# Two new step orders in the attention of an attention + squared-ReLU FFN kernel, with the spread sums as a step of their own and one head's scaled output by VectorE

## The chip, the cores and the metric

The kernel runs on one core of one Trainium2 chip. The metric is the device time of one execution in microseconds (us). Before the change three runs gave 1317.71, 1319.16 and 1319.85 us; the median is 1319.16 us. The core has five engines with an instruction queue each, which they work off strictly in order: TensorE (PE in the profile; PEld is its weight load), VectorE (DVE), ScalarE (ACT), GpSimd (POOL) and SyncE (SP), which here only issues DMAs. An instruction that needs another engine's result waits at the head of its queue, and all behind it waits too.

## The reference

Thresholded attention over 8 batches x 8 heads, 576 positions, head size 64, and then a two-layer FFN on 4608 tokens of width 512 with a hidden layer of 2048, all in float32:

```python
scores = scale * np.matmul(q, k.transpose(0, 1, 3, 2))
thresh = np.max(scores, axis=-1, keepdims=True) - tau
scores = np.where(scores >= thresh, scores, -1000000000.0)
scores = scores - np.max(scores, axis=-1, keepdims=True)
attn = np.exp(scores)
attn = attn / (np.sum(attn, axis=-1, keepdims=True) + 1e-09)
x = np.matmul(attn, v)            # heads of one batch side by side: (4608, 512)
h = np.maximum(x @ w_in, 0.0)
out = h * h @ w_out
```

The two weight arrays come in as 64-bit floats, so the kernel also turns them into 32-bit ones, with integer operations.

## The kernel before, in words

**Stages.** The attention fills the first 523 us of the profiled execution. The FFN follows; its layers use sums of blocks (a fast matrix product in two levels) and are not touched by the change.

**The unit of the attention** is one tile of 128 query rows of two heads (`units`, 144 of them; in two of nine, the 64 rows left over of two head pairs share a tile). Two units, A and B, make a period; there are 72 periods and a few more to fill and empty the pipeline. Each period does these steps; a step's name is the one in the order lists:

- `SA`, `SB`: score products of a unit with the first 512 keys, line 434 with 512 columns, in 64x64 tiles of TensorE. `RA`, `RB`: with the 64 keys left over, line 434 with 64 columns. They go to six PSUM banks of one tile `sc`: unit A to banks 0 and 5 and parts of 1 and 4, unit B to banks 2 and 3 and other parts of 1 and 4.
- `topA0` ... `topB1`: VectorE copies one head's 576 scores out of PSUM with the extremum (line 452). `leastA/B`: GpSimd makes the threshold (line 459). `powA0` ...: ScalarE's exponential (line 462). `maskA0` ...: VectorE's compare, multiply and row sum (line 467). `over`, `inv`: the sums plus 1e-9 on GpSimd (line 474) and their reciprocal on VectorE (line 477).
- `V`, `W`, `U`: TensorE transposes the masked weights, 64 rows at a time (line 380, tile form 64x128): 8 blocks of 18 in `V`, 2 in `W`, 8 in `U`, which is 16, 4 and 16 instructions. `V` and `U` go to the one two-bank PSUM buffer `pt`, `W` to banks 2 and 3 of `sc`. `W` also spreads the reciprocal sums over the rows with 8 small products (line 515, tile form 64x64). `eV`, `eW`, `eU`: ScalarE copies them out to SBUF (line 523).
- `PV`: the product with the values (line 532, tile form 64x64, 36 products of 128 columns, or the same in pieces), into banks 0 and 5. `x`: ScalarE copies the two heads' results out (line 658, 128x128 each). `xm`: GpSimd multiplies both by the spread reciprocal sums (line 664, 128x256), and SyncE stores them to DRAM.
- `T`: transposes of later queries (8 instructions) or keys (10), line 398, tile form 64x128, to the middles of banks 1 and 4, in most periods. `eT`: ScalarE takes them out (lines 403 and 411), and the next loads of queries or keys are issued.
- `c1` ... `c6`, `fetch`: the conversion of one block of FFN weights (line 205 on ScalarE, 212, 219 and 245 on GpSimd, 227 and 235 on VectorE) and its load. `s1`, `s2`: block sums of the first layer's weights on GpSimd.

**What sets the order.** Nothing schedules these steps: two lists written by hand, `CONVERTING` for the periods that convert weights (numbers 2 to 34) and `PLAIN` for the later ones, give the order in which every engine's queue receives them. Each `-` behind a name means one period earlier, so one pass of the list works on several periods at once. `run_period` walks a list; `BEGIN_WITH` has the lists of the first two periods. Between instructions on the same PSUM bank by different engines, `touch` adds a wait, even where they do not overlap. All instructions on a resource keep the order of the list.

Of the kernel before, what the change touches and what calls it, by code (L numbers as in the profile page):

```python
# [13 lines left out]
ALU = mybir.AluOpType  # L14
# [34 lines left out]
def kernel(  # L49
# [25 lines left out]
    nc = tc.nc  # L75
    B, H, S, D = q.shape
    P = 128
# [7 lines left out]
    BANK = 512  # L85
# [19 lines left out]
    ident = const.tile([P, P], FP32, name="ident")  # L105
# [168 lines left out]
    HALF = P // 2  # L274
# [80 lines left out]
    def touch(what, made, at, size, key=0):  # L355

        if at is None:
            return
        on = range(at // BANK, (at + size - 1) // BANK + 1)
        met = {made.ins.engine}  # L360
        for kind, other, others, its in reversed(touched):
            e = other.ins.engine
            if e == made.ins.engine:
                continue
            if on[-1] < others[0] or others[-1] < on[0]:
                if any({what, kind} == {x, y} and any((key - its) % n == 0 for n in rings) for x, y, rings in MEET):
                    continue
                tc.declare_no_dep(made.ins, other.ins, reason="other banks")
            elif e not in met:
                met.add(e)  # L370
                tc.add_manual_dep(made.ins, other.ins.name, behind, reason="same bank")
        touched.append((what, made, on, key))
        while len(touched) > 300:
            touched.popleft()

    def half_turn(pt, slot, of, at=None):

        for r in range(2):
            rows = ds(r * HALF, HALF)
            made = nc.tensor.transpose(pt[:, r, ts(slot, HALF)], of[rows, :], ident[rows, rows])  # L380
            touch("turns", made, at and at + r * BANK, BANK)
# [39 lines left out]
    soft, given, smalls = {}, deque(), {}  # L421
# [63 lines left out]
    wT = {}  # L485

    TURNS = {}
    for g in range(2, 2 * len(pairs)):
        two, x = divmod(g - 4, 4)
# [3 lines left out]
    FILLS = {"V": (0, 8), "W": (8, 2), "U": (10, 8)}  # L493
    SCALE_AT = 10
# [4 lines left out]
    def fill(m, f, pt, at=None):  # L499

        first, count = FILLS[f]
        if m not in wT:
            wT[m] = sb.tile([P, (2 * CH + 2) * P], FP32, tag="wT", bufs=W_RING, name="wT")
        for i, (u, c) in enumerate(FIRST[first : first + count]):
            half_turn(pt, i, weights[2 * m + u][:, c, :, :].rearrange("p j d -> p (j d)"), at)
        if f == "W":
            rs = smalls.pop(m)
            for j in range(2):
                for r in range(2):
                    rows = ds(r * HALF, HALF)  # L510
                    for u in range(2):
                        one = rs[rows, 3, 2 * u + j : 2 * u + j + 1]
                        wide = bass.AP(tensor=one.tensor, offset=one.offset, ap=[one.ap[0], [0, D]])
                        to = pt[ds(u * D, D), r, ts(count + j, HALF)]
                        made = nc.tensor.matmul(to, wide, ident[rows, rows], start=True, stop=True)
                        touch("turns", made, at and at + r * BANK, BANK)

    def filled(m, f, pt, at=None):

        first, count = FILLS[f]  # L520
        count += 2 * (f == "W")
        to = wT[m][:, ds(weight_at(first) * P, count * P)]
        touch("weights", nc.scalar.copy(joined(to), whole(pt, 0, count)), at, 2 * BANK, m)  # L523
# [35 lines left out]
    def has(n):  # L559
        return 0 <= n < NU  # L560
# [22 lines left out]
    def converts(p):  # L583
        return is_wide and (has_chunk(p) or has_chunk(p - 1))

    def has_chunk(p):
        return p in starts

    def begun(n):
        return starts.get(n)  # L590

    FIRST_PERIOD = -2
    PLAIN = """
        PV-- x-- V-- eV-- RA- c1- c3- inv-- W-- xm-- eW-- powB1-- c2 maskA0-- SA- maskA1-- U- c4 topA0- s1--
        powB0-- topA1- leastA- SB- eU- maskB1-- c6 RB- T- s2 maskB0-- eT- over- topB0- powA0- topB1- c5
        powA1- leastB- fetch
    """.split()
    CONVERTING = """
        RB- maskA0-- SA- maskA1-- inv-- powB1-- W-- U- topA0- eW-- c6- fetch topA1- leastA- SB- maskB0-- c1-
        c3- eT- maskB1-- topB0- c4 over- topB1- c2- leastB- eU- powA1- powA0- PV- c5 V- x- RA powB0- eV- T  # L600
        xm- s1 s2
    """.split()

    BEGIN_WITH = {
# [2 lines left out]
        maskB0 maskB1  # L607
        """.split(),
        1: """
        fetch SA RA RB SB T eT over topA0 topA1 leastA inv V topB0 topB1 leastB powA0 powA1 eV W powB0 eW  # L610
        maskA0 maskA1 powB1 maskB0 maskB1
        """.split(),
    }
# [7 lines left out]
    def period(p):  # L621

        A, B_, a, b = 2 * p, 2 * p + 1, 2 * p - 2, 2 * p - 1
        m, turns = p - 2, TURNS.get(p, ())
        late, pt = {"W": []}, {}

        def fills(f, m):
            if has(2 * m):
                pt[f] = pt_pool.tile([P, 2, BANK], FP32, tag="pt", name="pt")
                fill(m, f, pt[f])  # L630

        def evict(f, m):
            if has(2 * m):
                filled(m, f, pt[f], 2 * BANK if f == "W" else None)

        def W():
            if has(2 * m + 2):
                pt["W"] = middle()
                fill(m + 1, "W", pt["W"], 2 * BANK)

        def turn_some():
            free = None
            if turns and p < 2:
                pq = pt_pool.tile([P, 2, BANK], FP32, tag="pt", name="pq")
                free = [(pq[:, r, :], None) for r in range(2)]
            late["turn"] = [turn(g // 2, g % 2, free or spots()) for g in turns]

        def PV():
            if has(2 * m):
                values(m)  # L650

        def values_out():
            if not has(2 * m):
# [24 lines left out]

        def every(key):
            for then in late.get(key, ()):  # L680
                then()

        steps = {
            "U": lambda: fills("U", m), "V": lambda: fills("V", m + 1), "W": W, "T": turn_some,
            "eU": lambda: evict("U", m), "eV": lambda: evict("V", m + 1), "eW": lambda: evict("W", m + 1),
            "eT": lambda: every("turn"),
            "SA": lambda: scored(A), "SB": lambda: scored(B_),
            "RA": lambda: scored_rest(A), "RB": lambda: scored_rest(B_),
            "PV": PV, "x": values_out, "xm": given_out,
            "c1": lambda: convert1(begun(p)), "c2": lambda: convert2(begun(p)),  # L690
            "c3": lambda: convert3(begun(p)), "c4": lambda: convert4(begun(p - 1)),
            "c5": lambda: convert5(begun(p - 1)), "c6": lambda: convert6(begun(p - 1)),
            "s1": lambda: sums_due(p) and sums_step(), "s2": lambda: sums_due(p) and p < 60 and sums_step(), "fetch": lambda: fetch(begun(p + 2)),
        }
# [127 lines left out]
    both = arena[:, ds(X_AT[1], 2 * X_SIZE)].rearrange("p (s z) -> p s z", s=2)  # L822
# [525 lines left out]
```

## Time and profile before

| what | value |
|---|---|
| median of three runs | 1319.16 us (1317.71 to 1319.85) |
| the profiled execution's own time | 1316.8 us |
| its span, first to last instruction | 1315.0 us, so 1.8 us lie around it |
| TensorE's granted clock, mean | 0.997 |
| busy share of the span: PE, DVE, ACT, POOL | 98%, 75%, 65%, 78% |
| converting stretch, 33 to 250 us: PE, DVE, ACT, POOL busy | 211.64, 206.37, 202.92, 196.95 of 217 us |
| plain stretch, 264 to 490 us: the same | 225.91, 192.34, 205.80, 178.14 of 226 us |
| FFN, 523 to 1315 us: the same | 783.10, 526.75, 388.01, 621.13 of 792 us |

A busy TensorE in this table is not TensorE at its peak: its instructions are pipelined, and the end of each is modelled. Where one instruction starts against the one before it says more than the share.

### The profile page before, as it was taken

To read this page: it belongs to the slowest core of one execution; us is meant where nothing else is said; L and a number is where in the kernel's file an instruction comes from. 1 tells how busy PE (TensorE), PEld (TensorE's weight loads), DVE (VectorE), ACT (ScalarE), POOL (GpSimd) and SP (SyncE) were. 2 spreads that over 40 slices of the span, in tenths; PEclk is the share of its full clock that TensorE was granted. 3 is DMA by queue.
4 is the path that set the end of the run, shared out by engine and by line. 5 is a ranking of instruction groups with operands and counts; after the bars stand their busy time and mean duration, and the time that the engine had idled before them with its cause. 6 is when DMAs were issued, how large, how long until landed. Compare 5 with 4: busy or idle time off the path is not lost.

```text
span 1315.0 us, 46033 instructions
## 1 busy us (share of the span) xinstructions
PE 1292.6 (98%) x18287; PEld 1108.5 (84%) x18287; DVE 983.6 (75%) x2345; ACT 856.6 (65%) x1576; POOL 1030.5 (78%) x1070
## 2 busy tenths in 40 slices
PE   8999999999999999999999999999999999999998
PEld 5666666677777777988888888999999999999998
DVE  6999999988888886787786877867656654665463
ACT  6999999999999897476666766765524322432240
POOL 3989899888888653698897997958777777777775
PEclk8999999999999999999999999999999999999999
DMA  6655666443333311576768767769754134513511
GB/s 164 170 146 152 158 192 183 119 98 99 82 74 84 74 45 36 164 229 174 221 187 228 214 179 213 212 234 367 273 161 161 56 107 161 161 57 106 161 33 33
DMA packets 291417, 196.23 MB, mean 149 GB/s; under 512 B 100097, under 2 KB 252161, under 8 KB 291201
## 3 DMA queue, kind: packets, MB, share of 16 engines
q1 hardware_dynamic: 289888, 192.87, 51.0%
q8 instruction: 144, 2.36, 0.8%
q14 instruction: 73, 0.59, 0.1%
q10 hardware_dynamic: 1312, 0.41, 0.1%
HBM read 120.85 MB, written 72.35 MB: 147 GB/s over the span
## 4 chain that ended last, share of the span: by engine, by line
PE 54%; DMA 3%; ACT 2%; DVE 1%; issue 1%; SPq 1%; POOL 0%; ACTq 0%; DVEq 0%; POOLq 0%
PE po L1082 28%; PE ph L940 15%; PE ph L947 10%; DVE arena L125 1%; DMA g<-arena 1%; DMA wall<-w 1%; ACT c L796 1%; DMA arena<-xT 1%; SPq L778 1%; ACT arena L909 0%; DMA w<-arena 0%; ACT arena L910 0%; DVE arena L122 0%; PE sc L532 0%; ACT arena L523 0%
## 5 line engine op out<-in xcount | busy, mean ns | idle before, releaser
L125 POOL TENSOR_TENSOR arena<-arena 128x512 f32<-128x512 f32 (+1 forms) x314 | 378.0, 1222 | 138.0 <-DVE arena L125 107.8
L1082 PE MATMUL po<-wall,arena 128*128 128x128 f32 x3528 | 395.1, 275 | 2.3 <-ACT arena L757 2.0
L1082 PEld LDWEIGHTS po<-wall,arena 128*128 128x128 f32 x3528 | 394.4, 192 | 2.9 <-ACT arena L757 2.4
L125 DVE TENSOR_TENSOR arena<-ph,arena 128x512 f32<-128x512 f32 x378 | 255.3, 689 | 86.3 <-PE ph L940 30.7
L122 POOL TENSOR_TENSOR arena<-arena 128x128 f32<-128x128 f32 (+1 forms) x322 | 265.6, 827 | 25.3 <-DMA arena<-w 9.0
L940 PE MATMUL ph<-arena,wall 128*128 128x256 f32 x1176 | 256.8, 380 | 3.0 <-DVE arena L125 2.5
L940 PEld LDWEIGHTS ph<-arena,wall 128*128 128x128 f32 x1176 | 222.0, 190 | 37.4 <-DVE arena L125 7.6
L452 DVE TENSOR_SCALAR_CACHE_REDUCE arena<-sc 128x576 f32<-128x576 f32 x288 | 208.4, 753 | 51.0 <-ACT arena L523 36.3
L125 DVE TENSOR_TENSOR arena<-po,arena 128x128 f32<-128x128 f32 x378 | 108.3, 290 | 168.0 <-PE po L1082 163.0
L467 DVE SCALAR_TENSOR_TENSOR arena<-arena 128x576 f32<-128x576 f32 x288 | 223.1, 811 | 1.1 <-ACT arena L462 1.1
L796 ACT COPY c<-arena 128x512 f32<-128x512 f32 (+1 forms) x295 | 169.0, 578 | 74.5 <-DVE arena L122 35.8
L462 ACT ACTIVATE arena<-arena 128x576 f32<-128x576 f32 x288 | 213.3, 784 | 3.2 <-DVE arena L452 3.2
L434 PE MATMUL sc<-arena 64*64 64x512 f32 (+1 forms) x2304 | 195.6, 423 | 4.6 <-ACT arena L403 0.7
L532 PEld LDWEIGHTS sc<-arena 64*64 64x64 f32 x5760 | 148.6, 133 | 28.5 <-issue 13.0
L459 POOL TENSOR_SCALAR arena<-arena,tau_p 128x2 f32<-128x2 f32 x144 | 102.8, 714 | 87.2 <-DVE arena L452 56.6
L532 PE MATMUL sc<-arena 64*64 64x128 f32 (+1 forms) x5760 | 166.0, 262 | 2.6 <-ACT arena L523 0.8
L122 DVE TENSOR_TENSOR arena<-arena,c 128x512 f32<-128x512 f32 x235 | 154.4, 666 | 12.6 <-ACT c L796 8.7
L523 ACT COPY arena<-pt 128x1024 f32<-128x1024 f32 x144 | 145.7, 1012 | 9.3 <-PE pt L380 9.3
L757 ACT COPY arena<-po 128x128 f32<-128x128 f32 x63 | 16.7, 264 | 187.1 <-PE po L1082 183.7
L947 PE MATMUL ph<-arena,wall 128*128 128x128 f32 x1176 | 132.0, 275 | 0.7 <-ACT arena L658 0.7
L947 PEld LDWEIGHTS ph<-arena,wall 128*128 128x128 f32 x1176 | 131.6, 192 | 1.0 <-issue 0.8
L380 PEld LDWEIGHTS pt<-ident,arena 64*128 64x128 f32 x2304 | 83.5, 139 | 48.3 <-ACT arena L523 32.1
(53 smaller groups left out, 1154.2 us busy)
## 6 DMA issues: line engine op xcount, KB each, us to landing
arena<-g SPq DMA_DIRECT2D x144, 256.0 KB, 4.5
g<-arena SPq DMA_DIRECT2D x192, 128.0 KB, 2.9
w<-arena SPq DMA_DIRECT2D x60, 256.0 KB, 2.7
wall<-w SPq DMA_DIRECT2D x49, 256.0 KB, 5.4
g<-arena SPq DMA_DIRECT2D x48, 256.0 KB, 3.6
arena<-w SPq DMA_DIRECT2D x44, 256.0 KB, 3.3
arena<-in_v_dram SPq DMA_DIRECT2D x32, 288.0 KB, 4.2
out_dram<-arena SPq DMA_DIRECT2D x70, 128.0 KB, 2.5
```

What stands on the lines that cost most here:

```text
L122: e.tensor_tensor(out=out, in0=x, in1=y, op=ALU.subtract)
L125: e.tensor_tensor(out=out, in0=x, in1=y, op=ALU.add)
L434: made = nc.tensor.matmul(sc[at, ds(to, count)], lhs, kT[rows, ds(at_k, count)], start=True, stop=True)
L452: made = nc.vector.tensor_scalar(out=s[:, j, :], in0=sc[:, ds(at, S)], scalar1=1.0, scalar2=None, op0=ALU.mult, op1=ALU.min, accum_out=nmx ...
L462: nc.scalar.activation(out=w[:, :, j, :], in_=of(j), func=AF.Exp, bias=nmx[:, j : j + 1], scale=-1.0)
L467: nc.vector.scalar_tensor_tensor(out=w[:, :, j, :], in0=of(j), scalar=thr[:, j : j + 1], in1=w[:, :, j, :], op0=ALU.is_le, op1=ALU.mult, a ...
L523: touch("weights", nc.scalar.copy(joined(to), whole(pt, 0, count)), at, 2 * BANK, m)
L532: made = nc.tensor.matmul(sc[ds(u * D, D), ds(5 * j * BANK + row, count)], loaded_v[i][rows, (c - (u != j)) % CH, :], wT[m][rows, ds(weigh ...
L796: nc.scalar.copy(c, y)
L940: nc.tensor.matmul(to[:, 2 * j : 2 * j + 2, :], W_IN[m, k][:, ts(2 * h + j, P)], part_x(steps, k, m), start=(not more and j == 0), stop=Tr ...
L947: nc.tensor.matmul(to[:, j, :], W_IN[m, k][:, ts(j, P)], x, start=(not more and j == 0), stop=True, skip_group_check=True,)
L1082: nc.tensor.matmul(to, g[:, j, :], w[:, j, :], start=(not more and j == 0), stop=(j == 3), skip_group_check=True)
```

## The change

The change does four things.

- `PLAIN` and `CONVERTING` get new orders. In TensorE's queue the plain order was PV, V, RA, W with its sums, SA, U, SB, RB, T and is now U, SB, RB, PV, T, V, W, Q, SA, RA. The converting order was RB, SA, W with its sums, U, SB, PV, V, RA, T and is now RB, RA, PV, V, SA, T, W, Q, U, SB.
- The spread sums leave `fill` and become `spread_sums`, a step `Q` of its own.
- In plain periods the `x` of the second head is no longer copied by ScalarE: VectorE multiplies it out of PSUM by the spread reciprocal sums at once.
- GpSimd's `xm` in plain periods then covers the first head alone, 128x128. In converting periods `x` and `xm` are as before.

```diff
-        if f == "W":
-            rs = smalls.pop(m)
-            for j in range(2):
-                for r in range(2):
...
+    def spread_sums(m, pt, at):
+
+        rs, count = smalls.pop(m), FILLS["W"][1]
+        for j in range(2):
+            for r in range(2):
+                rows = ds(r * HALF, HALF)
+                for u in range(2):
+                    one = rs[rows, 3, 2 * u + j : 2 * u + j + 1]
+                    wide = bass.AP(tensor=one.tensor, offset=one.offset, ap=[one.ap[0], [0, D]])
+                    to = pt[ds(u * D, D), r, ts(count + j, HALF)]
+                    made = nc.tensor.matmul(to, wide, ident[rows, rows], start=True, stop=True)
+                    touch("turns", made, at + r * BANK, BANK)
...
     PLAIN = """
-        PV-- x-- V-- eV-- RA- c1- c3- inv-- W-- xm-- eW-- powB1-- c2 maskA0-- SA- maskA1-- U- c4 topA0- s1--
-        powB0-- topA1- leastA- SB- eU- maskB1-- c6 RB- T- s2 maskB0-- eT- over- topB0- powA0- topB1- c5
-        powA1- leastB- fetch
+        c5- U-- SB-- c6 c4- eU-- RB-- s1- PV-- powA0-- topB0-- over-- topB1-- c1 powA1-- c2- powB0--
+        maskA1-- T- x-- eT- leastB-- inv-- xm-- maskA0-- V-- W-- eV-- c3- Q-- eW-- powB1-- SA- maskB0-- RA-
+        s2- topA0- topA1- maskB1-- leastA- fetch
     """.split()
     CONVERTING = """
-        RB- maskA0-- SA- maskA1-- inv-- powB1-- W-- U- topA0- eW-- c6- fetch topA1- leastA- SB- maskB0-- c1-
-        c3- eT- maskB1-- topB0- c4 over- topB1- c2- leastB- eU- powA1- powA0- PV- c5 V- x- RA powB0- eV- T
-        xm- s1 s2
+        RB- RA eT- c5- topB1- powA0- c3- over- powA1- c6- fetch PV- x- powB1- c4 inv- topB0- leastB- V- eV-
+        SA T W- xm- maskA0- powB0- maskA1- topA0 Q- eW- topA1 c2- maskB1- c1 U eU maskB0- SB leastA s1 s2
     """.split()
...
-                touch("x", nc.scalar.copy(x[:, j, :], from_), 5 * j * BANK, P, m)
+                if converts(p) or j == 0:
+                    made = nc.scalar.copy(x[:, j, :], from_)
+                else:
+                    made = nc.vector.tensor_tensor(
+                        out=x[:, j, :], in0=from_, in1=wT[m][:, ts(SCALE_AT + j, P)], op=ALU.mult
+                    )
+                touch("x", made, 5 * j * BANK, P, m)
...
-                both = x[:, :, :].rearrange("p j n -> p (j n)")
-                nc.gpsimd.tensor_tensor(out=both, in0=both, in1=wT[m][:, ds(SCALE_AT * P, 2 * P)], op=ALU.mult)
+                made = x[:, 0 : 1 + converts(p), :].rearrange("p j n -> p (j n)")
+                scale = wT[m][:, ds(SCALE_AT * P, (1 + converts(p)) * P)]
+                nc.gpsimd.tensor_tensor(out=made, in0=made, in1=scale, op=ALU.mult)
```

In the list of the second starting period, `Q` stands behind `W`.

More of the change, by code (lines that the diff above doesn't have):

```diff
@@ L505, in fill @@
             half_turn(pt, i, weights[2 * m + u][:, c, :, :].rearrange("p j d -> p (j d)"), at)
-        if f == "W":
-            rs = smalls.pop(m)
-            for j in range(2):
-                for r in range(2):
[L510 to L516, printed above, removed]
+    def spread_sums(m, pt, at):
[9 more added lines that the diff above has]
+                    touch("turns", made, at + r * BANK, BANK)
     def filled(m, f, pt, at=None):
@@ L609 @@
         1: """
-        fetch SA RA RB SB T eT over topA0 topA1 leastA inv V topB0 topB1 leastB powA0 powA1 eV W powB0 eW
+        fetch SA RA RB SB T eT over topA0 topA1 leastA inv V topB0 topB1 leastB powA0 powA1 eV W Q powB0 eW
         maskA0 maskA1 powB1 maskB0 maskB1
@@ L639, in W, with Q @@
                 fill(m + 1, "W", pt["W"], 2 * BANK)
+        def Q():
+            if has(2 * m + 2):
+                spread_sums(m + 1, pt["W"], 2 * BANK)
         def turn_some():
@@ L683, in period @@
         steps = {
-            "U": lambda: fills("U", m), "V": lambda: fills("V", m + 1), "W": W, "T": turn_some,
+            "U": lambda: fills("U", m), "V": lambda: fills("V", m + 1), "W": W, "Q": Q, "T": turn_some,
             "eU": lambda: evict("U", m), "eV": lambda: evict("V", m + 1), "eW": lambda: evict("W", m + 1),
```

## The prediction

> **What bounds the kernel now.** I read first the busy time by stretch: 33 to 250 us are converting periods, 264 to 490 us plain ones, 523 us on is the FFN. Columns: stretch, its length, then busy us of PE, PEld, DVE, ACT and POOL, granted clock, DMA share, GB/s.
>
> ```profile
> 33.00:250.00 217.00, 211.64 (x5210) 146.29 (x5212) 206.37 (x575) 202.92 (x369) 196.95 (x212) 1.00 0.63 163
> 264.00:490.00 226.00, 225.91 (x5592) 162.59 (x5592) 192.34 (x553) 205.80 (x368) 178.14 (x186) 1.00 0.35 80
> 523.00:1315.00 792.00, 783.10 (x5880) 747.57 (x5878) 526.75 (x1054) 388.01 (x735) 621.13 (x625) 1.00 0.55 170
> ```
>
> In the plain stretch TensorE is never idle (225.91 of 226 us), the others are 79 to 91% busy. In the converting stretch four engines are busy 91 to 98%, and none is the plain limit. The FFN is not touched: its 792 us stay.
>
> Second, the order of time on PE over one plain period: start, us to the modelled end, line, shape, count.
>
> ```profile
> 402.11 0.71 PE L380 MATMUL pt<-ident,arena 64*128 64x64 f32 x16
> 402.76 0.34 PE L434 MATMUL sc<-arena 64*64 64x64 f32 x8
> 403.03 0.34 PE L380 MATMUL sc<-ident,arena 64*128 64x64 f32 x4
> 403.30 0.46 PE L515 MATMUL sc<-ident,arena 64*64 64x64 f32 x16
> 403.58 1.04 PE L434 MATMUL sc<-arena 64*64 64x512 f32 x8
> 404.55 0.71 PE L380 MATMUL pt<-ident,arena 64*128 64x64 f32 x16
> 405.20 1.37 PE L434 MATMUL sc<-arena 64*64 64x512 f32 x16
> 406.50 0.52 PE L398 MATMUL sc<-ident,arena 64*128 64x64 f32 x10
> 406.95 2.19 PE L532 MATMUL sc<-arena 64*64 64x128 f32 x72
> ```
>
> In starts these are V, RA, W, Q, SA, U, SB with RB, T, PV, and the next V stands at 409.08: a period of 6.97 us. A group's price is the distance to the next start: 16 transposes take 0.65, 4 take 0.27. So 12 more cost 0.38, one costs 0.032, four cost 0.127, and **0.143 us** are left over for each change between the tile forms 64*128 and 64*64. There is none inside a form: Q's start to SA's is 0.28 for 16 small products. The period has eight such changes, 1.14 us in which nobody else is waited for.
>
> Third, who waits for whom in the converting stretch and the plain one (us in total, times, longest), and in the order of time one converting loop on ACT:
>
> ```profile
> DVE arena L452 <- ACT arena L523: 8.6, 19, 0.7
> PEld sc L434 <- ACT arena L523: 7.7, 30, 0.3
> PEld sc L532 <- ACT arena L523: 6.9, 21, 0.4
> ...
> PEld sc L434 <- DVE arena L452: 9.4, 34, 0.3
> ```
>
> ```profile
> 152.98 0.59 ACT L523 COPY arena<-sc 128x512 f32<-128x512 f32 x1 [0.51 <-PE sc L515]
> 153.46 0.69 ACT L205 ACTIVATE arena<-arena 128x512 f32<-128x512 f32 x1
> 154.05 0.69 ACT L411 COPY arena<-sc 128x256 f32<-128x256 f32 x2
> 154.62 0.33 ACT L403 ACTIVATE arena<-sc,qscale 128x64 f32<-128x64 f32 x1
> 154.83 1.03 ACT L523 COPY arena<-pt 128x1024 f32<-128x1024 f32 x1
> 155.91 0.86 PEld L532 LDWEIGHTS sc<-arena 64*64 64x64 f32 x32 [0.35 <-ACT arena L523]
> ```
>
> Here TensorE does wait. eW (152.98) is followed on ScalarE by c1, eT and eU; the second half of PV waits for eU (155.91), then come V, RA, T, RB, SA, W, Q, and eW again at 160.24: 7.26 us a period, a loop through PE and ACT.
>
> **The change, part by part.** Periods: the copies of W (line 523, 128x512) number 30 in 217 us and 33 in 226 us, so 7.23 us converting and 6.85 plain; starts read off one by one give about 7.2 and 6.9, which I use. Some 31 converting periods and (510 - 264) / 6.9 = 36 plain ones are full.
>
> *Plain order, TensorE.* U | SB RB PV | T V W | Q SA RA: four changes of form where there were eight. 4 x 0.143 = 0.57 us less, 6.9 - 0.57 = 6.33 us, if nothing new is waited for. Three chains could prevent that; each is summed from starts above.
> - The bunch of evictions. V may be written only when U's copy is out, and the next U only when V's is, since pt is one buffer; T, V, W now come together, so eT, eV, eW stand together on ScalarE. U 0.65, SB and RB 1.30 - 0.14, PV 2.13, T 0.31 and 0.22 to its end, 0.04 to ACT's start, eT 0.79 (407.06 to 407.85), eV 1.01, 0.06 back to U: 6.37 us.
> - RA, then topA0 and topA1 (0.68 a step, 0.76 the last), then the second half of RB, which shares their banks: PV 2.13, T 0.31, V 0.51, W 0.27, Q and SA 1.11, RA 0.34, start 0.12, tops 1.44, back 0.05, half of RB 0.06: 6.34 us. This wait is in the trace already (9.4 us, 34 times).
> - VectorE's sum: 192.34 / 33 = 5.83, and x.
>
> All three come out at the new PE sum, so I allow 0.07 us for waits that alternate between them and take 6.40. Bounds: 6.33, and 6.9 if they eat it all. Gain 0.50 x 36 = **18 us** (bounds 0 to 20.5).
>
> *x of the second head.* ScalarE loses the later half of a pair: 0.43 for two copies against 0.27 for one, 0.16 us. VectorE gets a product of 128x128 out of PSUM; the same shape from PSUM in the FFN (line 125) takes 0.29. VectorE comes to 6.1 us, ScalarE from 205.80 / 33 = 6.24 to 6.1: both under 6.33, so hidden. In VectorE's queue x stands behind maskA1 and ahead of inv, maskA0, maskB0. RA's end to maskA1's end is 0.12 + 4 x 0.68 + 2 x 0.74 = 4.3 us, PV ends about 4.0 after U's start: its input is there, so those three are not held up. Without that cover it would cost its 0.3.
>
> *xm.* GpSimd's 128x256 takes 1.20; 128x128 lies between its 128x2 (0.83) and that; the FFN's 128x128 rows say 0.83. Minus 0.37 of 5.4 us, off the path: nothing. Stores of x wait for two engines now, and SyncE's loads of q and k stand behind them; those are asked for two head pairs (9 periods) ahead and land in some 4 us: nothing.
>
> *Converting order.* RB RA PV | V | SA | T W | Q | U | SB: six changes for eight, 0.29 us of TensorE. More important is that the loop above is cut: eT moves to the front, and eU is followed by SB, RB and RA before PV wants it. The next limits: VectorE's sum, 206.37 us in 30 periods, 6.88; and SB 0.91, RB and RA 0.24, PV 2.19, 0.12, x 0.33, powB1 0.70, eV 0.93, powB0 0.70, eW 0.59 and 0.07 back to SB: 6.78. Bounds 6.88 and 7.2. I take 6.93, nearer the floor, for the one reason that periods without T run at 6.76 already, so four full engines can. Gain 0.27 x 31 = **8.4 us** (bounds 0 to 10). c1 to c6 and fetch only move within a period or one period on; four raw buffers cover a load that has 12 us to land. W's sums as Q cost the same products.
>
> *Sum.* 18 + 8.4 = 26.4 us off the profiled 1316.8 us (span 1315.0 and 1.8 around it): 1290.4. The median of the runs lies 2.4 above that execution, so **1292.8 us** against 1319.16.
>
> [...] In the trace VectorE's masks of two SBUF operands start at 402.92, 406.10 and 406.84, and end 0.81 later, while GpSimd operations that started at 403.12 (1.20 long), 406.28 (0.79) and 407.04 (1.75) run beside them. [...]
>
> **The rivals.**
> - *Plain only* (chance 0.15). The converting loop is replaced by another of 7.2; four engines at 91% and more speak for it, the 6.76 against. 1319.2 - 18 = 1301.
> - *Converting only* (0.08). The plain chains, all within 0.05 of each other, fill up to 6.9. 1319.2 - 8.4 = 1311. Against it: each holds only work of fixed length.
> - *Slower: ScalarE's train closes a loop* (0.12). In plain periods powB1 stands behind eT, eV, eW; maskB1 waits for powB1, topB0 stands behind maskB1, powB0 waits for topB0, and x and the next eT stand behind powB0. Bare: 0.78 + 0.74 + 0.76 + 0.68 + 0.27 + 0.79 + 0.93 + 0.48 and three handovers of 0.06 are 5.6 us. With 0.7 of waits in it, it binds; from 1.5 on (7.1 a period) it takes back the converting gain too. At 7.4: 36 x 0.5 - 8.4 = 10 slower, 1329. For it: eT, eV and eW each wait for their own TensorE group. Against: these are done 0.5 us before their turn by the first chain.
> - *GpSimd and VectorE set the period, or the changes of form cost nothing* (0.04). 1319. Against: 226 us without a PE gap, and the masks above.
>
> **Chances and range.** The forecast has 0.61 and its own range is 1283 to 1303 (6.33 to 6.55 plain, 6.88 to 7.05 converting). A measurement here can tell about 0.2%, 2.6 us. Faster 0.61 + 0.15 + 0.08 = 0.84, same 0.04, slower 0.12. The range for 8 in 10 takes in both rivals on the faster side: 1281 to 1314.
>
> **What would show it.** Right: in the plain stretch four form changes a period, U starts about 6.4 us apart; 39 products of VectorE out of sc at 0.29, 105 copies of x left on ScalarE; converting periods at 6.9 with VectorE 98% busy; the FFN at 792 us. Wrong: TensorE gaps before U on eV, or before RB on topA1, of more than 0.2 us; VectorE idle before topA0 in converting periods as now; a change of form that costs less than 0.14 when groups are longer.

## The result and the profile after

The changed kernel takes 1296.95 us (median of four runs, 1293.16 to 1298.73); the kernel before, on the same chip, 1319.51 us. The ratio is 0.9828, 95% interval 0.9803 to 0.9852: 22.6 us less. The profiled execution took 1296.16 us with a span of 1294.2 us, 20.6 and 20.8 us less than the one of before. The forecast was 1292.8 us, with a range of 1281 to 1314.

The same three stages in the trace after (columns as in the prediction; the FFN now begins at 503.3 us instead of 522.7):

```profile
33.00:250.00 217.00, 207.26 (x5176) 146.14 (x5174) 210.75 (x569) 203.15 (x368) 203.74 (x211) 1.00 0.60 164
264.00:490.00 226.00, 225.03 (x6066) 171.23 (x6066) 220.65 (x639) 212.87 (x357) 173.60 (x197) 1.00 0.36 83
503.30:1294.00 790.70, 783.20 (x5880) 748.01 (x5880) 526.28 (x1054) 387.72 (x735) 620.36 (x625) 1.00 0.55 170
```

The FFN did not change (790.7 us). The plain stretch holds 6066 matmul records in 226 us where it held 5592. In the converting stretch TensorE's count is the same (5176 against 5210) and VectorE is now the fullest engine.

The long waits of TensorE's weight loads in the converting stretch, 33 to 240 us (us in total, times, longest):

```profile
PEld sc L398 <- DVE arena L452: 21.8, 24, 1.0
PEld sc L434 <- DVE arena L452: 12.1, 42, 0.5
PEld sc L434 <- ACT arena L525: 9.2, 29, 1.7
```

VectorE's waits of the operations of line 452 for ScalarE's copies (line 523, now 525), 7.4 us in the same 207 us before, are down to a single one of 1.4. The longest waits are now put down to VectorE. The first row is not all lost time: it is T's weight load, which stands behind SA's products, and in the period of 182.60 below T starts at 184.83, where SA's products end (184.90). The second is mostly RB's wait for the top operations.

Period by period, by the starts of `inv` (line 477), this is sharper. The 36th `inv` starts at 270.9 us before and at 270.7 after: up to there nothing was gained. The 65th starts at 472.0 before and 456.1 after: 29 plain periods of 6.94 us became 29 of 6.395. The usual converting period went from 7.25 to 7.13 us. But the few short ones of 6.76 us, one for each T that is missing, are gone as well, and the mean had been 7.20 with them; and two long ones (9.24 and 8.78) are in this trace, which cost some 3.5 us.

One plain period after, in the order of time on PE (start, us to the modelled end):

```profile
404.49 0.53 PE L398 MATMUL sc<-ident,arena 64*128 64x64 f32 x10
404.85 0.66 PE L380 MATMUL pt<-ident,arena 64*128 64x64 f32 x16
405.35 0.29 PE L380 MATMUL sc<-ident,arena 64*128 64x64 f32 x4
405.57 0.46 PE L517 MATMUL sc<-ident,arena 64*64 64x64 f32 x16
405.85 1.16 PE L434 MATMUL sc<-arena 64*64 64x512 f32 x16
406.93 0.71 PE L380 MATMUL pt<-ident,arena 64*128 64x64 f32 x16
407.57 1.31 PE L434 MATMUL sc<-arena 64*64 64x512 f32 x14
...
408.78 2.13 PE L534 MATMUL sc<-arena 64*64 64x128 f32 x70
410.84 0.71 PE L380 MATMUL pt<-ident,arena 64*128 64x64 f32 x16
```

V, at 404.85, is followed by W in the same tile form: 16 transposes take 0.50 us to the next start. U, at 406.93, is followed by products in the other form: the same 16 transposes take 0.64. The difference, 0.14 us, is the prediction's price of a change of form, here inside one period; they are the usual distances of all 29 plain periods between 270 and 455 us. The rest of the period fits too. Set against the period that the prediction shows (both have ten transposes in T), T, V and W, which stood alone before, now take 1.08 instead of 1.37 us, SA with RA 1.08 instead of 0.97 + 0.27, and SB, RB and PV 3.27 instead of 1.30 + 2.13. That is 0.29, 0.16 and 0.16 us, for two, one and one change of form, and Q and U take what they took; together they are the step from 6.97 to 6.35.

The same period on DVE and POOL. DVE's rows are, in order, maskA1, x, inv, maskA0, maskB0 and the next topA0; POOL's are leastB, xm and a block sum.

```profile
404.22 0.81 DVE L467 SCALAR_TENSOR_TENSOR arena<-arena 128x576 f32<-128x576 f32 x1
...
404.96 0.28 DVE L666 TENSOR_TENSOR arena<-sc,arena 128x128 f32<-128x128 f32 x1
...
405.16 0.17 DVE L477 RECIPROCAL arena<-arena 128x4 f32<-128x4 f32 x1
405.20 0.90 POOL L459 TENSOR_SCALAR arena<-arena,tau_p 128x2 f32<-128x2 f32 x1
405.24 0.79 DVE L467 SCALAR_TENSOR_TENSOR arena<-arena 128x576 f32<-128x576 f32 x1
...
406.07 0.45 POOL L676 TENSOR_TENSOR arena<-arena 128x128 f32<-128x128 f32 x1
406.14 1.00 DVE L467 SCALAR_TENSOR_TENSOR arena<-arena 128x576 f32<-128x576 f32 x1
...
406.49 1.79 POOL L122 TENSOR_TENSOR arena<-arena 128x512 f32<-128x512 f32 x1
...
407.11 0.76 DVE L452 TENSOR_SCALAR_CACHE_REDUCE arena<-sc 128x576 f32<-128x576 f32 x1
```

VectorE has hardly a gap, and its masks do not all last the same: maskB0 took 1.00 us, and it started 0.07 us after xm of GpSimd. This is not by chance. maskB0 needs the threshold that leastB makes, and waits for it here: leastB ends at 406.10, and maskB0 starts at 406.14, 0.90 us after maskA0, where one mask follows another in 0.74 elsewhere. The next operation in GpSimd's queue, xm, starts at the same moment. In 26 plain periods of this trace maskB0 started 0.03 to 0.04 us after the end of leastB and 0.06 to 0.07 us after the start of xm. The block sum behind xm took 1.79 us; where no mask stood in its way, it took 1.28. This pair of rows is where the prediction went wrong, and most of the experiments turn on it.

### The profile page after: what moved, and what is told of

Read it like the earlier page. It is cut to its first block, busy times and chain, and to the rows that moved or that the text cites. A ratio compares the mean times of both kernels' runs of the same rounds, so it can differ in the third digit from the quotient of the medians.

```text
span 1294.2 us, 46028 instructions
## 1 busy us (share of the span) xinstructions
PE 1267.6 (98%) x18287; PEld 1103.2 (85%) x18287; DVE 1000.9 (77%) x2384; ACT 848.7 (66%) x1537; POOL 1022.8 (79%) x1070
## 4 chain that ended last, share of the span: by engine, by line
PE 68%; DVE 10%; DMA 7%; ACT 7%; issue 5%; POOL 2%; SPq 1%; DVEq 0%; ACTq 0%; POOLq 0%
PE po L1094 28%; PE ph L952 13%; PE sc L434 7%; PE ph L959 7%; PE sc L534 6%; DVE arena L452 4%; PE pt L380 3%; DVE arena L467 3%; DMA wall<-w 2%; ACT arena L525 2%; PE sc L398 1%; ACT arena L462 1%; PE sc L517 1%; DMA arena<-g 1%; DMA g<-arena 1%
## 5 line engine op out<-in xcount | busy, mean ns | idle before, releaser
L467 DVE SCALAR_TENSOR_TENSOR arena<-arena 128x576 f32<-128x576 f32 x288 | 238.7, 848 | 3.4 <-ACT arena L462 0.5
L462 ACT ACTIVATE arena<-arena 128x576 f32<-128x576 f32 x288 | 216.0, 795 | 4.0 <-DVE arena L452 3.8
L434 PE MATMUL sc<-arena 64*64 64x512 f32 (+1 forms) x2304 | 188.2, 418 | 7.9 <-ACT arena L403 1.5
L459 POOL TENSOR_SCALAR arena<-arena,tau_p 128x2 f32<-128x2 f32 x144 | 124.7, 866 | 78.4 <-DVE arena L452 71.5
L534 PEld LDWEIGHTS sc<-arena 64*64 64x64 f32 x5760 | 150.4, 133 | 0.9 <-issue 0.4
L434 PEld LDWEIGHTS sc<-arena 64*64 64x64 f32 x2304 | 78.5, 133 | 83.5 <-issue 35.4
```

Source lines behind the costliest of these rows:

```text
L434: made = nc.tensor.matmul(sc[at, ds(to, count)], lhs, kT[rows, ds(at_k, count)], start=True, stop=True)
L462: nc.scalar.activation(out=w[:, :, j, :], in_=of(j), func=AF.Exp, bias=nmx[:, j : j + 1], scale=-1.0)
L467: nc.vector.scalar_tensor_tensor(out=w[:, :, j, :], in0=of(j), scalar=thr[:, j : j + 1], in1=w[:, :, j, :], op0=ALU.is_le, op1=ALU.mult, a ...
L534: made = nc.tensor.matmul(sc[ds(u * D, D), ds(5 * j * BANK + row, count)], loaded_v[i][rows, (c - (u != j)) % CH, :], wT[m][rows, ds(weigh ...
```

## What the experiments were to tell apart

The theory that came out of these rows, called *the lock* here: where a mask or c5 (VectorE operations with two inputs from SBUF) and a GpSimd operation on SBUF meet, the later one waits for the earlier one, and its recorded time contains the waiting. In the rows above, maskB0 takes 1.00 us with 0.38 us of xm left at its start, and maskA0 0.79; leastB takes 0.90 beside maskA0, where the same operation took 0.29 with no mask near it (10.73 us in this trace); and the block sum takes 1.79 beside maskB0 instead of 1.28. (Starts some hundredths apart do not tell the order: in the rows above, leastB starts 0.04 us ahead of maskA0 and is the one that waits.) The rival is the prediction's own reading, that the engines run side by side and each has its own sum. The first runs ask the plainer question, which part of the change brought the time. Ratios are to the kernel before on the same chip.

### The plain order alone

```diff
     CONVERTING = """
-        RB- RA eT- c5- topB1- powA0- ...
+        RB- maskA0-- SA- maskA1-- inv-- powB1-- W-- Q-- U- ...   (the order of before, Q behind W)
```

> The new plain order with VectorE's x, but the old converting order (Q directly behind W in it). Theory P (the whole gain is the plain order's): as the changed kernel or a little better, 1295 to 1299 us, plain periods at 6.36 and converting ones at 7.25 and 6.76 as before. Rival B (both orders gave some, as the prediction's sum has it, 18 and 8.4): 1301 to 1303.

Measured: 1297.02 us, ratio 0.9846 (0.9830 to 0.9863); usual converting periods 7.25, plain periods 6.405 on average. All of the gain, within what can be told, is the plain part's.

### The converting order alone

```diff
     PLAIN = """
-        c5- U-- SB-- c6 c4- eU-- ...
+        PV-- x-- V-- eV-- RA- c1- c3- inv-- W-- Q-- xm-- ...   (the order of before)
-                if converts(p) or j == 0:
+                if True:
```

(and xm of 128x256 in all periods)

At the hand-over from one list to the other, one turn of queries or keys is overwritten in this kernel before it is taken out; the instructions are the same ones.

> The new converting order, but the old plain order (Q directly behind W in it) with both x copies by ScalarE. Theory P: no gain, 1317 to 1321 us, with converting periods at 7.13. Rival B: 8 us faster, 1311.

Measured: 1315.03 us, ratio 0.9988 (0.9974 to 1.0001); converting periods 7.14, plain 6.93. The converting order is worth about 2 us (0 to 3.4 by the interval), not 8.4: between the two theories, and nearer the first. It did cut the loop through TensorE and ScalarE that the prediction had found, but a new limit stands 0.12 us behind it, and it holds the periods without T as well, which took 6.76 before.

### More changes of form: V behind Q

```diff
-        maskA1-- T- x-- eT- leastB-- inv-- xm-- maskA0-- V-- W-- eV-- c3- Q-- eW-- powB1-- SA- ...
+        maskA1-- T- x-- eT- leastB-- inv-- xm-- maskA0-- W-- c3- Q-- V-- eV-- eW-- powB1-- SA- ...
```

> The changed kernel, but in plain periods V stands behind Q, so that a period has six changes of tile form instead of four; ScalarE's order and all the work are the same. Theory T (TensorE binds the plain periods and a change of form costs 0.143): 2 x 0.143 x 36 = 10 us more than the changed kernel, about 1307. Rival D (VectorE, 98% busy there now, binds, and the changes of form are free in this order): at most 3 us more, 1297 to 1300. Rival A (what hurts is ScalarE's bunch of evictions eT, eV, eW waiting): more than 15 us more.

Measured: 1323.64 us, ratio 1.0043 (1.0026 to 1.0061); plain periods 6.97. This is 27 us more than the changed kernel. Only the theory of ScalarE's bunch had more than 15, but the rows of this run name another cause:

```profile
403.15 0.32 PEld L517 LDWEIGHTS sc<-ident,arena 64*64 64x64 f32 x16 [0.25 <-DVE arena L477]
...
403.54 0.71 PE L380 MATMUL pt<-ident,arena 64*128 64x64 f32 x16
...
404.18 1.20 PE L434 MATMUL sc<-arena 64*64 64x512 f32 x16
404.35 1.01 ACT L525 COPY arena<-pt 128x1024 f32<-128x1024 f32 x1 [0.48 <-PE pt L380]
...
405.50 0.76 DVE L452 TENSOR_SCALAR_CACHE_REDUCE arena<-sc 128x576 f32<-128x576 f32 x1 [0.57 <-ACT arena L525]
```

Q waits for inv. topA0's wait is put down to eV, but nothing in the program makes topA0 wait for that copy; RA, whose scores it needs, ends within 0.02 us of it (405.38 and 405.36), so I take RA, which stands behind V, to be what it waits for. ScalarE is not the limit: it stands idle for 0.48 us ahead of eV. So topA0, topA1, maskB1, topB0, topB1, maskA1, x and inv (4.4 us on VectorE) and then Q, V, SA and RA make a loop of 6.97 us, and V's 0.64 us was put inside it. So this run doesn't price a change of form. That price stands on the rows of plain periods above, not on an experiment of its own.

### x of both heads by ScalarE again

```diff
-                if converts(p) or j == 0:
+                if True:
...
-                made = x[:, 0 : 1 + converts(p), :].rearrange("p j n -> p (j n)")
+                made = x[:, 0:2, :].rearrange("p j n -> p (j n)")
```

> The changed kernel, but the second head's x is copied by ScalarE and multiplied by GpSimd in plain periods, as before. Theory T (TensorE binds): 0 to 3 us more than the changed kernel, 1297 to 1300, since VectorE's 0.2 and ScalarE's 0.16 both lie beside TensorE. Rival D (VectorE binds the plain periods): 0.2 x 36 = 7 us less, 1290. Rival G (GpSimd or ScalarE would bind without the relief): more than 5 us more.

Measured: 1301.98 us, ratio 0.9890 (0.9866 to 0.9913); plain periods 6.60. Moving x is worth 5 us by the medians, 6 to 8 by the ratios and 7.5 by the periods (0.21 us in 36 of them), where the prediction had nothing, although VectorE was given more to do. Only the third theory had the size, and its reason, a GpSimd or ScalarE that is full, is not what the rows show; xm is now 128x256, and maskB0 starts 0.06 us behind it:

```profile
401.49 0.72 POOL L676 TENSOR_TENSOR arena<-arena 128x256 f32<-128x256 f32 x1
401.55 1.28 DVE L467 SCALAR_TENSOR_TENSOR arena<-arena 128x576 f32<-128x576 f32 x1
```

maskB0 takes 1.28 instead of 1.00, since xm holds it off for 0.72 instead of 0.45. The rest balances: x's 0.20 us are gone from VectorE, but inv then waits about as long (0.19) for `over`. 6.32 - 0.20 + 0.19 + 0.27 = 6.58, the usual period of this run.

### Both copies by ScalarE and no xm in plain periods

```diff
+                if converts(p):
                     nc.gpsimd.tensor_tensor(out=made, in0=made, in1=scale, op=ALU.mult)
```

(on top of the kernel with x of both heads by ScalarE; the outputs of plain periods are then not divided by their sums)

> Plain periods with both copies of x by ScalarE and GpSimd's multiplication xm left out (so x of these periods is not divided by its sums). To be read against the kernel with both copies by ScalarE and xm of 128x256, which had plain periods of 6.58 and a ratio of 0.989. Theory L: maskB0, recorded there with 1.28, falls to 0.81, and the period to TensorE's own sum, 6.30 to 6.36; ratio 0.981 to 0.984. The rival, that the 8 us came from ScalarE's second copy and its train, or from the gap in front of inv: maskB0 may fall, but the period stays at 6.5 to 6.6, ratio 0.987 to 0.990.

Measured: 1314.93 us, ratio 0.9978 (0.9966 to 0.9990); plain periods 7.13. Both expectations missed: taking an operation *away* from GpSimd, which is busy 144 of 220 us in this stretch, cost 12 to 13 us against the kernel with xm. The rows:

```profile
406.84 1.27 POOL L122 TENSOR_TENSOR wall<-wall 128x512 f32<-128x512 f32 x1
...
406.91 1.82 DVE L467 SCALAR_TENSOR_TENSOR arena<-arena 128x576 f32<-128x576 f32 x1
```

With xm gone, the block sum s2 is next behind leastB in GpSimd's queue. It starts 0.07 us ahead of maskB0 and holds it off for its whole 1.27 us, so the mask's record grows to 1.82. It is 0.55 us more than with xm; in the 24 plain periods that have an s2 that makes 13 us: the loss. In the late periods without s2 this kernel falls to 6.05 us without T, and to 6.1 and 6.35 to 6.7 by turns with it. I had asked only what xm would no longer block, not what would come forward in its place. A reading in which the engines run side by side has no place for a mask of 1.82 us.

### GpSimd's load in converting periods

```diff
-                made = x[:, 0 : 1 + converts(p), :].rearrange("p j n -> p (j n)")
+                made = x[:, 0:1, :].rearrange("p j n -> p (j n)")
```

(xm then covers the first head alone in converting periods too, and the second head's division is left out there)

> The changed kernel, but in converting periods GpSimd multiplies only the first head's x (128x128 instead of 128x256); the second head's output is not divided by its sums there, so that part of the computation is left out. Theory G (in converting periods GpSimd's queue, worked off without a gap, holds the period at 7.13, through over, for which inv waits): some 0.3 us a period less, 31 x 0.3 = 9, about 1288. Rival D (VectorE, 97% busy there, holds it): at most 2 us less, 1295 to 1297.

Measured: 1296.44 us, ratio 0.9836 (0.9807 to 0.9864); converting periods 7.14. So the amount of GpSimd's work is not what holds these periods. leastA's record, 1.13 us in the changed kernel, grew to some 1.43: what GpSimd saved, it spent waiting behind maskB1, maskB0 and c5.

### x of the second head by VectorE in converting periods too

```diff
-                if converts(p) or j == 0:
+                if j == 0:
```

(with xm of 128x128 in all periods)

> The changed kernel, but VectorE makes the second head's x in converting periods too, and GpSimd's product is 128x128 there too. GpSimd gets 0.75 us a period less, ScalarE 0.16 less, VectorE 0.2 more. Theory G (GpSimd holds the converting periods): faster, 3 to 8 us, 1289 to 1294. Rival D (VectorE holds them): 0.2 x 31 = 6 us more, 1303.

Measured: 1297.49 us, ratio 0.9844 (0.9816 to 0.9872); converting periods 7.185. Neither theory had that. VectorE was given 0.2 us more and the period grew by 0.05; xm was made shorter, which by the run before this one buys nothing here, where hardly a mask starts while it runs.

### over, inv and topB0 ahead of c3 and c4

```diff
-        RB- RA eT- c5- topB1- powA0- c3- over- powA1- c6- fetch PV- x- powB1- c4 inv- topB0- ...
+        RB- RA eT- c5- topB1- powA0- over- c3- powA1- c6- fetch PV- x- powB1- inv- topB0- c4 ...
```

> The changed kernel, but in converting periods over stands ahead of c3 in GpSimd's queue, and inv and topB0 ahead of c4 in VectorE's. Same work. Theory O (VectorE loses about 0.3 us a period because inv waits for over, which stands behind c3): 0.2 to 0.3 us a period less, 6 to 9, 1288 to 1291. Rival S (GpSimd's sum sets the period, its order does not matter): no change, 1295 to 1298.

Measured: 1306.25 us, ratio 0.9911 (0.9879 to 0.9943); converting periods 7.47. The same instructions in nearly the same order cost about 9 us more. c6 now meets c4, and the whole of xm meets maskA1:

```profile
160.20 1.04 POOL L245 TENSOR_TENSOR arena<-arena 128x512 int32<-128x512 int32 x1
...
160.79 0.73 DVE L227 TENSOR_SCALAR arena<-arena 128x512 int32<-128x512 int32 x1
...
161.65 1.20 POOL L676 TENSOR_TENSOR arena<-arena 128x256 f32<-128x256 f32 x1
162.19 1.28 DVE L467 SCALAR_TENSOR_TENSOR arena<-arena 128x576 f32<-128x576 f32 x1
```

c4 took 0.73 instead of 0.43, the mask 1.28 instead of 0.81. What I expected here of `over`, and the rival with the sum of GpSimd, both fell.

### The lock in the converting order: topB1 ahead of c5

By now the converting period of the changed kernel could be read with the lock. DVE's rows are topB1, c4, inv, topB0 and maskA0, and later maskB0 and c5; POOL's are c3, over and c6, and later leastA. The rows of the other engines are left out.

```profile
182.60 0.75 DVE L452 TENSOR_SCALAR_CACHE_REDUCE arena<-sc 128x576 f32<-128x576 f32 x1
182.74 0.61 POOL L219 TENSOR_SCALAR arena<-arena 128x512 f32<-128x512 f32 x1
183.38 0.43 DVE L227 TENSOR_SCALAR arena<-arena 128x512 int32<-128x512 int32 x1
183.42 0.47 POOL L474 TENSOR_SCALAR arena<-arena 128x4 f32<-128x4 f32 x1
183.93 0.18 DVE L477 RECIPROCAL arena<-arena 128x4 f32<-128x4 f32 x1
183.97 1.04 POOL L245 TENSOR_TENSOR arena<-arena 128x512 int32<-128x512 int32 x1
184.02 0.73 DVE L452 TENSOR_SCALAR_CACHE_REDUCE arena<-sc 128x576 f32<-128x576 f32 x1
184.67 0.95 DVE L467 SCALAR_TENSOR_TENSOR arena<-arena 128x576 f32<-128x576 f32 x1
...
188.39 0.81 DVE L467 SCALAR_TENSOR_TENSOR arena<-arena 128x576 f32<-128x576 f32 x1
188.78 1.13 POOL L459 TENSOR_SCALAR arena<-arena,tau_p 128x2 f32<-128x2 f32 x1
189.13 0.71 DVE L235 SCALAR_TENSOR_TENSOR arena<-arena 128x512 int32<-128x512 int32 x1
```

leastA (188.78), a tiny operation, is kept out by maskB0 and c5 and lasts 1.13 us. c3 behind it ends just ahead of c4, `over` (0.47, 0.23 elsewhere) is kept out by c4, inv comes late, c6 starts late and holds off maskA0 (0.95). None of this shows as a wait on a semaphore.

```diff
-        RB- RA eT- c5- topB1- powA0- c3- over- powA1- ...
+        RB- RA eT- topB1- c5- powA0- c3- over- powA1- ...
```

> Converting list with topB1 ahead of c5 on VectorE, nothing else moved. Theory L (a VectorE operation with two SBUF inputs, a mask or c5, and a GpSimd operation on SBUF exclude each other; a GpSimd record holds its waiting): in the changed kernel leastA stands on GpSimd behind maskB1, maskB0 and c5 in a row and is recorded with 1.13 us, and c3, over, c4 and inv come late behind it. With topB1 in between it should end some 0.6 us earlier, its record should fall to 0.5 to 0.9, c4 should no longer wait for c3; over may then be kept out by c5. Period 7.13 to between 6.85 and 7.02, 4 to 9 us less than the changed kernel, ratio to before 0.976 to 0.980. Theory A (the engines run beside each other, and the period is set by the sum of VectorE or by a loop through TensorE): the same work in nearly the same order, 7.1 to 7.15, ratio 0.982 to 0.984.

Measured: 1293.98 us, ratio 0.9817 (0.9793 to 0.9840). The converting period fell from 7.13 to 6.98, inside the lock's range; leastA's record fell to 0.61. The ratio is a little above the range given, and its interval overlaps the changed kernel's, so this comparison was made again, below.

### c3 behind xm, c4 ahead of c5

```diff
-        RB- RA eT- c5- topB1- powA0- c3- over- powA1- c6- fetch PV- x- powB1- c4 inv- topB0- ...
+        RB- RA eT- c4- c5- topB1- powA0- over- powA1- c6- fetch PV- x- powB1- inv- topB0- ...
-        SA T W- xm- maskA0- powB0- maskA1- topA0 Q- eW- topA1 c2- maskB1- ...
+        SA T W- xm- maskA0- powB0- maskA1- topA0 Q- eW- topA1 c3- c2- maskB1- ...
```

(and in the plain list c4 ahead of c5, for the last block)

> Converting list with c3 moved on GpSimd from behind leastA to behind xm, and c4 put right ahead of c5 on VectorE, of the same block, so that topB1, inv, topB0 follow in a row with leastA, over and c6 of GpSimd beside them, and xm and c3 beside topA0 and topA1. Theory L: bare durations fit those two stretches but for some 0.1 to 0.2 us each (leastA 0.2, over 0.23, c6 1.04 against 1.45 us; leastB 0.2, xm 0.72, c3 0.61 against 1.36), no wait of c4 for c3 or of inv for over; maskA0 and maskB1 wait 0.1 to 0.2 each. Period 6.85 to 7.0, ratio 0.975 to 0.980. Theory A: the same sums on each engine, 7.1 to 7.15, ratio 0.982 to 0.984.

Measured: 1300.75 us, ratio 0.9864 (0.9844 to 0.9883); converting periods 7.28. Both ranges were missed. The waits of c4, inv and maskA0 went as expected, but maskB1 lost more than they gave:

```profile
166.87 0.61 POOL L219 TENSOR_SCALAR arena<-arena 128x512 f32<-128x512 f32 x1
...
167.56 1.61 POOL L212 TENSOR_SCALAR arena<-arena 128x512 int32<-128x512 uint32 x1
167.60 1.24 DVE L467 SCALAR_TENSOR_TENSOR arena<-arena 128x576 f32<-128x576 f32 x1
```

c3 was over in time. c2, pushed back behind it, starts 0.04 us ahead of maskB1 and keeps it out. I had taken c2 for harmless, since masks that start in its later part last 0.81. It is harmless only there: the 29 masks of this run that started with 1.5 us or more of c2 left lasted 1.19 to 1.32, and the masks of the changed kernel that started with 1.04 us or less of it left lasted 0.81 or 0.82. So c2 holds the way for about the first 0.65 us of its 1.61: an estimate, from the 1.24 us of this mask, the 0.04 us by which c2 started ahead of it, and the 0.61 us by which masks outlast xm and c6 in the other runs.

### A wait taken away that should be worth nothing

The lock makes a sharp prediction where a plain reading of the waits makes another: inv waits 0.07 us for `over` in the kernel with topB1 first. Moving inv out of the way should gain nothing, because the mask behind it is released by c6.

```diff
-        ... PV- x- powB1- c4 inv- topB0- leastB- V- eV-
+        ... PV- x- powB1- c4 topB0- inv- leastB- V- eV-
```

> The kernel with topB1 ahead of c5, and inv moved from ahead of topB0 to behind it, so that VectorE no longer waits for over there (0.07 us a converting period; what needs inv, the spread sums, comes 0.5 us later). Theory L: maskA0 ends when c6 has ended and 0.61 us are over, and c6 starts when over has ended, which c5 and c4 keep out; none of that moves, so maskA0 starts earlier and lasts longer, and the period stays at 6.98 (6.96 to 6.99). Theory A (VectorE's own sum and its visible waits): 6.91, 2 us less. Beside the changed kernel on the same chip: 4 to 6 us less by the period (0.15 us in 31 periods), the changed kernel's single long periods apart.

> The changed kernel as it is, beside the one with topB1 ahead of c5 and inv later, to compare the two on one chip in five rounds. By its first trace: converting periods 7.13, plain periods 6.32, ratio to before 0.982 to 0.985.

Measured on one chip: with topB1 first and inv later 1292.50 us, ratio 0.9803 (0.9789 to 0.9817); the changed kernel again 1296.89 us, ratio 0.9845 (0.9831 to 0.9858). The period stayed at 6.98:

```profile
167.42 1.04 POOL L245 TENSOR_TENSOR arena<-arena 128x512 int32<-128x512 int32 x1
...
167.97 1.10 DVE L467 SCALAR_TENSOR_TENSOR arena<-arena 128x576 f32<-128x576 f32 x1
```

maskA0 starts earlier and lasts 1.08 to 1.10 (28 periods of 31) instead of 0.95. The lock's forecast held, the other fell. And the two moved words make a kernel that is 4.4 us faster than the changed one, with intervals that do not touch.

## Why the prediction was right, and where it was wrong

**The plain order: right, in size and by its step.** 18 us were forecast, with periods of 6.40; the trace has 6.395, and the plain order alone brings 20.3 us (1317.35 to 1297.02). The working was four changes of form less at 0.143, a TensorE sum of 6.33. The rows of the kernel without xm, in its late periods, bear this out: there a period with ten transposes in T takes 6.35 us on TensorE from its first transpose to the next, one without T 6.04. Of the three chains that the prediction summed to 6.34 to 6.37, the first shows no wait of V or U for a copy of pt, and the second only the waits of at most 0.3 us that it had before. What it didn't see is that VectorE stands at 6.32 as well, and not at the 6.1 that it had added up: its steps undisturbed are 4 x 0.74 + 4 x 0.68 + 0.28, 5.96 us, and some 0.16 of waiting for leastB and 0.23 of waiting for xm come on top, both at maskB0. That the price of a change of form is what brought the gain rests on these rows, not on a run that changes nothing else.

**x on VectorE, "hidden", and the smaller xm, "off the path: nothing": wrong.** The durations of x were right (0.28 for 0.29), that of xm was not (0.45 for 0.83, which is the mean of line 122's two shapes on GpSimd; its 128x128 rows alone take 0.46 in the trace before). The step that failed is the cover. xm is off the path only as long as no mask starts while it runs; maskB0 and xm both stand behind leastB, and so the mask starts right behind xm in the plain periods. The pair of moves is worth 5 to 8 us, a quarter to a third of the result; had the kernel kept both copies on ScalarE, the forecast of 6.40 would have missed at 6.60.

**The converting order: right in mechanism, mis-sized: 8.4 us forecast, about 2 measured.** The loop through TensorE and ScalarE was there and was cut. The wrong term is the next limit, taken as 6.93 from VectorE's sum of 6.88 and from periods without T that "run at 6.76 already". Those take 7.13 now like the rest, so what they had less of, T and its copies, is not what sets the period now. The limit was 7.13: VectorE's operations undisturbed come to about 6.75 us there, and 0.15 at maskA0, 0.1 at c4 and 0.1 to 0.2 at inv are added by the lock (c4 and inv wait for c3 and `over`, which it has made late). The run with topB1 first, which moves nothing but one operation, took 0.15 us of that back.

**The masks beside GpSimd operations: misread.** The prediction set masks that last 0.81 beside GpSimd operations against the rival that GpSimd and VectorE set the period. Those masks had started first; it was GpSimd that paid: the xm quoted there took 1.20 us, and 0.72 where it started ahead of the mask, with x of both heads by ScalarE. The rows of the converting stretch, before and after (line 219 is c3, count, then busy us and mean ns), show the payment:

```profile
L219 POOL TENSOR_SCALAR arena<-arena 128x512 f32<-128x512 f32 x28 | 30.3, 1081 | 0.0
```

```profile
L219 POOL TENSOR_SCALAR arena<-arena 128x512 f32<-128x512 f32 x28 | 18.0, 643 | 0.0
L467 DVE SCALAR_TENSOR_TENSOR arena<-arena 128x576 f32<-128x576 f32 x116 | 93.7, 842 | 0.0
```

c3, the same operation on the same tile, took 1.08 us every time before and 0.61 in most periods after. The masks (line 467) went the other way, from a mean of 811 ns to 842. Of GpSimd's busy time before, then, a good part was waiting. Its 5.4 us in a plain period (178.14 / 33) and four masks of 0.81 add up to 8.6 us in a period of 6.9; that sum counts the waiting twice. Undisturbed, a plain period needs 4 x 0.74 for the masks, 2 x 1.28 for the sums, 0.45 for xm and 0.23 for over, 6.2 us one after the other (the two small thresholds left out), which fits in 6.32. How long a mask is held off fits to about 0.01 us: with 0.34 (c6) and 0.39 us (xm) left at their start in the trace after, 0.47 (c6, with inv later), 0.66 (xm, with x by ScalarE again) and 1.21 (s2, without xm) of a two-input GpSimd operation, masks lasted 0.95, 1.00, 1.09, 1.28 and 1.82, each 0.61 or 0.62 more than what was left. The top operations, which read PSUM, did not pay: 0.72 to 0.77 in the trace after, beside whatever ran. c4, with one input from SBUF, did, beside c6 (0.73 for 0.43, with `over` first). And c2 held masks off for some 0.65 us of its 1.61 only. Why the two engines hold each other off was not shown.

**The rivals.** "Plain only", given 0.15 and 1301, was nearest in its kind: the loop was replaced by another limit of nearly the old length, though by VectorE's queue and not by four full engines. By its time alone the result cannot be told from the forecast: 1297 lies halfway between the two. The slower rival, ScalarE's train, did not appear. "GpSimd and VectorE set the period", given 0.04, was wrong on the time and half right on the mechanism. The total landed within 4 us of the forecast partly by luck: the converting term was 6 us short, and the plain term, some 2 us better than forecast, took part of that back. Within the plain term there was luck as well, since the move of x and the shorter xm, which were given nothing, kept it from missing by 5 to 8 us.

## What to carry to other kernels

Read an operation's duration against the shortest one of its kind before you add up an engine's busy time: here two values for one shape (c3 with 1.08 and 0.61 us, a mask with 0.81 and 1.82) meant that a wait was hidden in the record. Where a trace shows such pairs, lay GpSimd's operations under those VectorE operations that do not pay (here the top operations, 0.72 to 0.77 us beside whatever ran), and ask of every operation that you remove or shorten on GpSimd which one will come forward and start just ahead of the next mask. Here that was whatever stood behind leastB, since the mask that needs leastB's result starts at the same moment (0.06 to 0.07 us behind xm, and 0.07 behind s2 in the run without xm). A wait that is shown on a semaphore is not worth its length if the instruction behind it is held by something else, as with inv's 0.07 us here: without that wait the period stayed at 6.98.

## What the runs showed of the hardware that was not expected

- A mask that starts while GpSimd runs a two-input operation, with 0.23 us or more of it left, ends 0.61 to 0.62 us after that operation, whatever its size (xm, c6 and the block sums: 0.85 us with 0.23 of c6 left in the trace before, 1.82 with 1.21 of s2 left in the run without xm; with 0.12 us of a block sum left it still lasts 0.81 in the trace after); 0.07 us of difference in starting time decides whether a mask takes 0.81 or 1.82 us.
- c2 (a one-input GpSimd operation from unsigned to signed integers, 128x512, 1.61 us) keeps masks out only in its first 0.65 us or so. Why was not tried.
- Single converting periods 1 to 3.5 us longer than the others appear in most of the profiled executions with the new plain order (9.24 and 8.78 after, 9.27 in its second trace, 10.58 with x by ScalarE, 10.20 with inv later), mostly the 20th and the 28th. There are none in the trace before and none with the old plain order and the new converting one, but hardly one with topB1 first either (7.32). In the trace after, TensorE stands still for 1.69 us between PV and V in the first of them and for 0.86 us in the middle of SA's products in the second, without a wait of its products that the trace names. They are worth up to 5 us in an execution; their cause stays open.
